# An attention and MLP block on one core: 84 five-pattern tiles made of two patterns, and nearly all shifts put on GpSimd in batches

## The chip, the cores and the metric

The program runs on one NeuronCore of a Trainium2 chip. The metric is the device time of one execution in microseconds. The engines are called as in the profile: PE (TensorE), ACT (ScalarE), DVE (VectorE), POOL (GpSimd) and SP (SyncE, which issues most DMAs). Each runs its own list of instructions in order, and they wait for each other by semaphores.

## The reference

One block with two branches on the same normalised input: attention with 32 query heads of width 16 that share one key and one value head, and an MLP with a tanh GELU. There are 2048 rows of width 512; the MLP is 1792 wide.

```python
xn = _layernorm(x)
q = (xn @ wq).reshape(B, S, 32, 16).transpose(0, 2, 1, 3)
k, v = xn @ wk, xn @ wv
p = softmax(einsum("bhqd,bkd->bhqk", q, k) * 16 ** -0.5)
attn = einsum("bhqk,bkd->bhqd", p, v).transpose(0, 2, 1, 3).reshape(B, S, 512) @ wo
h = gelu(einsum("bsd,df->bsf", xn, w1) + b1)
out = x + attn + einsum("bsf,fd->bsd", h, w2) + b2
```

## The kernel before

**Tiles and units.** The scores are cut into 2048 tiles of 128 keys by 512 queries, one PSUM bank each. Three tiles make a unit; there are 683 units. PSUM holds two halves of three banks: while the tiles of one unit are turned into exponentials out of one half, PE writes the scores of the next unit into the other (L1069, three matmuls that take one 32-row group of the array each, so that they run together). A half is written again when every tile in it has been read.

**Two ways to an exponential.** A table of 683 letters (DTAB) says which tiles of a unit go to ACT and which to DVE. ACT reads its one to three tiles of a unit with one Exp (L1109) into the buffer E. DVE reads a tile with one instruction, called p1 in the code (L1140): it adds a constant to the f32 score, cuts it off at 64 and writes int16. Read as bf16, these bits are a rough exponential: the upper bits are the power of two, and the lower seven a straight line in place of the curve. The error is smoothed by summing five patterns: the same bits with -26, 0, 26, 51 and 77 added (SPL_K), each weighted by a constant that is put into its own copy of V (SPL_C, V1). So a tile of DVE costs four shifts, each an integer addition on a whole tile, and five matmuls with V where a tile of ACT costs one. The bits and their shifted copies lie in the buffer Dt: 19 places for first bits, and three times 11 for copies.

**Batches.** Up to six tiles of DVE are gathered, and then `close_batch` writes their shifts (L1182 to L1197). SPL_STEPS says for each kind of batch which shift goes to which engine: "p" is POOL, in pieces of at most two tiles (PL_N, L1186), with a 64-bit integer addition that treats four int16 at a time; "d" is DVE, over all tiles of the batch (L1193). A piece meant for POOL is done by DVE (L1161) where the planner finds that earlier (L389 to L393). The planner starts POOL's pieces only beside DVE instructions that aren't marked `lock` (L384 to L398).

**The products with V** (`pv_mm`, L1153) use 32 columns of the array each, so four run side by side, one per head of a group. They add into bank 6; bank 7 takes the projections of q, the MLP and the output projection in pieces, four column groups side by side as well (L749, L767) or as row pieces that ride on the score matmuls (L763).

**What sets the order.** The whole program is recorded first, and `Prog.schedule` then plays it through with costs of its own and writes the order of each engine. Its tables set costs (C_OCC, PL_OCC), due times of the side work (HP, YP, QK, Q3) and, for the preparation, the order of its instructions (PRO_DUE). `emit` adds a semaphore wait wherever an instruction needs another engine's result. The order is therefore fixed when the program is built; on the chip only the waits move.

**Stages.** Preparation (layer norm, transposes, k, v, the first q) until the first Exp; then the 683 units with all the side work between them, and two stretches in which ACT does GELUs (L1342, L1347); then the end: the last output rows (`y_last`, `o_norm_last`) and one store.

Of the kernel before, what the change touches and what calls it, by code (L numbers as in the profile page):

```python
# [5 lines left out]
dt = mybir.dt  # L6
# [31 lines left out]
P1_ALLOW = -20.0  # L38
EV_ALLOW = -2.0
S_WAIT = 0.1  # L40
P_WAIT = 0.0
PL_OCC = (0.398, 0.61)
PL_N = 2
ON_OCC = 0.66
PL_LAT = 0.06
PL_GATE = 0.1
PL_WIN = 0.4
PL_TAKE = 1.0
PL_DUE = 3.0
PL_START = 0.065  # L50
PL_SEM = 0.16
PL_FREE = 0.06
# [3 lines left out]
RH = ((0,0,1,1,0,0,1,0,1,1,0,1,0,1),(0,0,0,0,1,1,1,1,1,1,1,1,1,1),(0,1,0,0,1,0,0,1,1,0,0,0,2,0),(1,0,0,1,0,1,1,1,1,1,1,1,1,1))  # L56
RQ = ((1,1,1,1),(0,0,2,2),(1,0,2,2),(0,0,0,0))
RY = ((4,3,3,4),(4,3,4,2),(4,5,2,3),(4,4,2,5))
# [13 lines left out]
DMASK = {".": (), "0": (0,), "2": (2,), "a": (0, 1), "b": (1, 2), "x": (0, 1, 2),  # L72
         "o": (0,), "t": (2,), "A": (0, 1), "B": (1, 2), "X": (0, 1, 2),
         "p": (0,), "u": (2,), "C": (0, 1), "D": (1, 2), "Y": (0, 1, 2)}
CLOSE = "otABXpuCDY"
THREE = "puCDY"
DTAB = "o0t02o.Ct0u2...0p00o.u2..p00po0t00p0tu0202....2uttt2tu0..C.o202p.222t.0oo0pt.B.0upp.p.2o2p22.2p000pp2.22p0o2t222.uo00p000u2t2o022tt2t2u20.2p0o02222.u220u000u0u0o02o202o2o..2u0t0t2uttbXXxXDu2u.20u0p0o02p222puo02.A202.tu0p0p.ap.0up0oo0p.0u0t020u.p.0ob.22.a002.p.b.B2.t.up2.otpt02.C0.p0p0.o020u0p0t2utt2.2p0o0p.t0t0o0o0o00o.202ut.0p0t200p0pt2.u2u020uu2p2u0u0.02p2u20002o2p002.u0ut020o0.o000.u020p20ou.ooo2t..u0u.p22u2p.p.B2pb.2u2po0p2put0pp00u2p0o..22.oo..2u020p0op22222p..2u2p2u020p2t022t2t.2o0022u000.0p2t0o0puu0pbYxYYA2t2p2t2.o0t0t202220u2po220tpp0.0202p.2p0p022p2p0u0p200ut2u000.p020u0o2022p2o00.2p202utp0p2t0tpu0t0t.u..0pt0uo0p2ppu0o2ptoo.pt..uo0oppa.p2.p.pp.ppup...bb.t000tt.tp..."
YF = 671.2567
# [11 lines left out]
Q3 = (3.13604,15.59782,1.3122)  # L90
QK = ((79.39235,91.86289,161.48976),(89.43004,105.17994,147.29074),(107.14608,109.54065,152.86984))
HP = ((35.0394,106.61171,41.40498,24.75776,42.85696,74.69052,118.31736,29.75129,84.77514,90.16891,73.93822,12.90461,18.00252,59.26326),(53.1749,30.86375,13.60201,93.43062,56.91912,0,0,0,0,0,0,0,0,0),(249.98302,265.3673,301.57062,267.28344,332.95778,255.58795,276.31909,268.60694,288.87995,299.75237,231.3787,266.76069,464.96186,415.4469),(420.73779,406.30738,480.5553,448.48685,406.52914,0,0,0,0,0,0,0,0,0))
YP = ((216.91445,183.61894,219.257,200.80829),(342.24149,390.93758,358.11329,404.06844),(569.56343,516.05804,661.62593,615.81662),(590.23906,607.46323,652.09363,671.23592))
# [36 lines left out]
class Prog:  # L130
# [131 lines left out]
    def schedule(self):  # L262
# [12 lines left out]
        able = dict(ready)  # L275
# [34 lines left out]
        while left:  # L310
            best_e, best_t = None, None
            for e in engs:
# [3 lines left out]
                if not able[e] and not pro:  # L316
                    continue
# [1245 lines left out]
```

## Time and profile before

| | us |
|---|---|
| median of 3 runs | 719.8 (719.77 to 720.71) |
| span of the profiled execution | 718.4 |
| busy: PE, DVE, ACT, POOL | 705.1, 701.2, 704.2, 446.1 |
| ACT, all Exp instructions (L1109), 675 of them | 652.6 |
| DVE, p1 (L1140), 589 of them | 409.5 |
| DVE, shifts planned for it (L1193) and taken from POOL (L1161) | 155.9 and 96.3 |
| POOL, shifts (L1160), 659 of them | 424.1, idle ahead of them 251.2 |

The profile is of one execution, and its span is 1.4 us below the median of the runs. Busy time is what an engine spent on its instructions; on ACT and DVE an instruction's record overlaps the next one's by some 0.08 to 0.25 us, so what one costs is the distance from its start to the next one's. On PE four column matmuls run at once, and each record is about 0.38 us long though the next four start after 0.22. POOL's records include the time that an instruction stands still after its start.

### The profile page before, as it was taken

The numbers are of one execution on the slowest core, as the hardware profiler recorded it, in microseconds if no ns is written. First come the engines' busy times: TensorE is split into PE (matmuls) and PEld (weight loads), VectorE is DVE, ScalarE is ACT, GpSimd is POOL, SyncE is SP. The second block draws the span as 40 slices with busy tenths as digits, with TensorE's granted clock in tenths as the row PEclk, the third lists the DMA queues.
The fourth block names the chain that finished last, engine by engine and source line by source line (L and its number), as shares of the span: only waits on it lengthen the run. The fifth ranks groups of instructions, "written<-read, shape, count | busy, mean of one in ns | idle before, by whom it ended". The sixth has DMA issues, their size and how long they took to land.

```text
span 718.4 us, 22628 instructions
## 1 busy us (share of the span) xinstructions
PE 705.1 (98%) x9241; PEld 220.3 (31%) x9244; DVE 701.2 (98%) x1396; ACT 704.2 (98%) x761; POOL 446.1 (62%) x727
## 2 busy tenths in 40 slices
PE   7899999999999999999999999999999999999998
PEld 4332333222233233322322233232234222222332
DVE  8899999999999999999999999999999999999996
ACT  7899999999999999999999999999999999999997
POOL 8355555777665654566776754746875766765431
PEclk9999999999999999999999999999999999999999
DMA  9200100101020010110101011010110101111111
GB/s 302 86 10 17 33 10 18 26 10 25 13 41 20 18 39 17 23 42 16 26 18 32 24 40 26 21 22 15 28 24 18 19 22 26 32 23 31 28 30 41
DMA packets 36255, 23.60 MB, mean 33 GB/s; under 512 B 17768, under 2 KB 32568, under 8 KB 36152
## 3 DMA queue, kind: packets, MB, share of 16 engines
q1 hardware_dynamic: 34824, 21.86, 12.1%
q8 instruction: 74, 1.21, 0.7%
q10 hardware_dynamic: 1328, 0.30, 0.2%
q14 instruction: 29, 0.24, 0.1%
HBM read 13.28 MB, written 2.35 MB: 22 GB/s over the span
## 4 chain that ended last, share of the span: by engine, by line
ACT 49%; PE 46%; DVE 3%; DMA 1%; issue 0%; SPq 0%
ACT E L1109 49%; PE pAll L1153 23%; PE pAll L1085 14%; PE pAll L767 5%; PE pAll L749 3%; DVE stats L857 1%; DVE Dt L1140 1%; DMA x_sb<-in_A_x_dram 1%; DVE ub L894 0%; PE pAll L1523 0%; DVE xnT L920 0%; DVE ub L1319 0%; PE pAll L763 0%; DVE mv L871 0%; DVE Dt L1193 0%
## 5 line engine op out<-in xcount | busy, mean ns | idle before, releaser
L1109 ACT ACTIVATE E<-pAll 128x1024 bf16<-128x1024 f32 (+2 forms) x675 | 652.6, 1150 | 1.9 <-PE pAll L763 0.8
L1160 POOL INT64_ADD Dt<-Dt x659 | 424.1, 652 | 251.2 <-DVE Dt L1140 84.9
L1140 DVE TENSOR_SCALAR Dt<-pAll 128x512 int16<-128x512 f32 (+1 forms) x589 | 409.5, 713 | 5.8 <-PE pAll L763 3.8
L1153 PE MATMUL pAll<-Dt,V 128*32 128x512 bf16 x3120 | 414.0, 383 | 0.1
L1153 PE MATMUL pAll<-E,V 128*32 128x512 bf16 x1424 | 281.2, 385 | 0.0
L1085 PE MATMUL pAll<-QT,KT 32*128 32x512 bf16 x2048 | 266.9, 384 | 4.1 <-ACT E L1109 2.8
L1193 DVE TENSOR_SCALAR Dt<-Dt 128x1024 int16<-128x1024 int16 (+6 forms) x286 | 155.9, 556 | 0.3
L1085 PEld LDWEIGHTS pAll<-QT,KT 32*128 32x128 bf16 x2048 | 66.6, 90 | 275.5 <-ACT E L1109 258.5
L1153 PEld LDWEIGHTS pAll<-Dt,V 128*32 128x32 bf16 x3120 | 106.1, 94 | 111.6 <-issue 79.8
L1161 DVE TENSOR_SCALAR Dt<-Dt 128x1024 int16<-128x1024 int16 (+1 forms) x294 | 96.3, 357 | 0.0
L1153 PEld LDWEIGHTS pAll<-E,V 128*32 128x32 bf16 x1424 | 64.5, 94 | 48.5 <-issue 37.6
L767 PE MATMUL pAll<-xnT,w_sb 128*32 128x512 bf16 x544 | 78.0, 383 | 0.3 <-DVE ub L1319 0.3
L767 PE MATMUL pAll<-w_sb,ub 128*32 128x512 bf16 x336 | 51.2, 381 | 0.0
L763 PE MATMUL pAll<-w_sb,ub 32*128 32x512 bf16 x112 | 43.1, 384 | 0.1
L767 PE MATMUL pAll<-w_sb,x_sb 128*32 128x512 bf16 x300 | 42.8, 382 | 0.0
L767 PE MATMUL pAll<-wop,oTp 128*32 128x512 bf16 x192 | 36.2, 382 | 0.0
L763 PE MATMUL pAll<-w_sb,x_sb 32*128 32x512 bf16 x92 | 35.4, 384 | 0.0
L767 PEld LDWEIGHTS pAll<-xnT,w_sb 128*32 128x32 bf16 x544 | 20.4, 94 | 13.8 <-issue 8.4
L763 PE MATMUL pAll<-xnT,w_sb 32*128 32x512 bf16 x64 | 24.6, 384 | 0.0
L1319 DVE TENSOR_SCALAR ub<-pAll,b1T 128x512 bf16<-128x512 f32 x28 | 20.7, 740 | 0.1
L763 PE MATMUL pAll<-xnT,wq_sb 32*128 32x512 bf16 x52 | 20.0, 384 | 0.0
L749 PE MATMUL pAll<-xnT,w_sb 128*32 128x512 bf16 x288 | 18.8, 380 | 0.0
(135 smaller groups left out, 352.5 us busy)
## 6 DMA issues: line engine op xcount, KB each, us to landing
w_sb<-in_B_w_dram SPq DMA_DIRECT2D x2, 1792.0 KB, 14.1
OfP<-Of SPq DMA_DIRECT2D x96, 32.0 KB, 2.0
rbP<-rden_rows SPq DMA_DIRECT2D x96, 32.0 KB, 1.9
x_sb<-in_A_x_dram SPq DMA_DIRECT2D x16, 128.0 KB, 2.2
QT<-qp SPq DMA_DIRECT2D x124, 16.0 KB, 1.8
out_dram<-x_sb SPq DMA_DIRECT2D x15, 128.0 KB, 1.7
x_sb<-in_A_x_dram SPq DMA_DIRECT2D x7, 256.0 KB, 5.5
OfP<-Of SPq DMA_DIRECT2D x56, 16.0 KB, 1.9
```

Source lines behind the costliest of these rows:

```text
L749: add("pe", lambda e, c=c, j=j: e.matmul(o[c, :], l[:, c], rh, start=start, stop=stop, tile_position=(0, 32 * j)), r, [(k, j) for k in w] ...
L763: add("pe", lambda e, b, c=c, j=j: e.matmul(pM, l[c, :], rh[c, :], start=False, stop=b, skip_group_check=True, tile_position=(32 * j, 0)), ...
L767: add("pe", lambda e, b, c=c, j=j: e.matmul(pM[c, :], l[:, c], rh, start=n == 0, stop=b, skip_group_check=True, tile_position=(0, 32 * j)) ...
L857: dve(lambda e, ti=ti, c=c: e.bn_stats(stats[:, c, :], x_sb[:, ti, :]), r=[("x", ti)], w=[("st", ti)], n=511)
L1085: ins = e.matmul(o, l, rh, start=True, stop=True, tile_position=(q0, 0))
L1109: o = act(lambda e: e.activation(E[:, s0:s0 + na, :], bank(b0, na).rearrange("p (a n) -> p a n", a=na), ACT.Exp, scale=LN2 / 128.0), w=[B( ...
L1140: op = dve(lambda e: e.tensor_scalar(Dt[:, s:s + n, :], bank(bk, n).rearrange("p (a n) -> p a n", a=n), float(127 * 128) + SPL_D, SPL_MIN, ...
L1153: add("pe", lambda e, a, b: e.matmul(pO[32 * j:32 * j + 32, :], V1[:, v, kt, :], rhs, start=a, stop=b, tile_position=(0, 32 * j)), r=r + [ ...
L1160: return e.int64_add(d.bitcast(dt.uint64), x.bitcast(dt.uint64), k * 0x0001000100010001 % 2 ** 64)
L1161: return e.tensor_scalar(d, x, float(k), None, ALU.add)
L1193: dve(lambda e, d=view(o, nb), q=view(i, nb), k=k: e.tensor_scalar(d, q, float(k), None, ALU.add), r=keys(i), w=keys(o), n=nb * n * TBW, m ...
L1319: dve(lambda e: e.tensor_scalar(ubs[tb % 2][:, ft, :], pM, b1T[:, ft:ft + 1], None, ALU.add), r=["b1T"], w=M4 + [ukey(tb, ft)], n=TBW + 57 ...
```

## The change

**Two patterns.** Batches whose letter in the new table BTAB is S, T or U (39 batches, 84 tiles) are made another way. p1 adds another constant. Then DVE writes two parts of the bits with bit operations: the mantissa bits with a fixed exponent, a number m between 0.5 and 1, and the exponent bits alone, a power of two P. One product puts (first bits) x m in the place of the first bits. The sum of P and that product, 2^e (1 + (1 + f)^2 / 2), is the exponential up to a constant factor and a small error, so two matmuls with the plain V take the place of five. The other 544 tiles of DVE keep five patterns.

**All shifts on POOL.** The new SPL_STEPS give every shift to POOL but for 15 instructions of the kind "d" in the third variant. PL_N is 6, and a step may cover two neighbouring copies, so one POOL instruction now takes one to twelve tiles. DVE no longer takes shifts from POOL.

**Tables and planner.** DTAB, and with it the split between ACT and DVE, is new (ACT has 1420 tiles instead of 1424). PTAB sets the priority of each p1. A `lock` instruction of DVE is planned outside POOL's instructions; the first POOL instruction after one waits for it by a semaphore, but no `lock` instruction of DVE waits for POOL on that account. A few costs, the due times, and the order of the preparation are new.

```diff
-SPL_STEPS = (((1, 0, 1, 26, "p"), (2, 0, 2, 51, "d"), (0, 0, 1, -26, "p")),
-             ((1, 0, 1, 26, "p"), (2, 0, 1, 51, "d"), (3, 0, 1, 77, "p"), (0, 0, 1, -26, "p")))
+SPL_STEPS = (((1, 0, 1, 26, "p"), (2, 0, 1, 51, "p"), (3, 0, 1, 77, "p"), (0, 0, 1, -26, "p")),
+             ((1, 0, 1, 26, "p"), (2, 0, 2, 51, "p"), (0, 0, 1, -26, "p")),
+             ((1, 0, 1, 26, "p"), (2, 0, 2, 51, "d"), (0, 0, 1, -26, "p")))
+POST = (1.0, -1.0, 4.0)
+P1 = {".": -20.0, "a": 0.0, "b": 0.4, "c": 1.0}
+QUAD = 18
+QUAD_TS, QUAD_TT = 4, 2
+QUAD_D = 127 * 128 - 75.0461
...
-C_OCC = 0.197
+C_OCC = 0.2075
...
-PL_OCC = (0.398, 0.61)
-PL_N = 2
+PL_FIX, PL_TILE, PL_N = 0.1635, 0.2124, 6
...
         def seen(o):
             if o.kind == "rs":
                 return o.rdy + RS_MAX
-            return max(o.rdy + (PL_TAKE if o.kind == "pl" else 0.0), lockend) if o.lock else o.rdy
+            return max(o.rdy, dlock if o.eng == "pool" else lockend) if o.lock else o.rdy
...
-                if e == "dve" and op.kind == "pl":
-                    ready["pool"].remove(op)
-                    ready["dve"].append(op)
-                    op.eng = op.stream = "dve"
...
+                if e == "pool" and op.lock:
+                    if any(o.lock and o.rdy + LK_WAIT <= t for o in ready["dve"]):
+                        free["pool"] = max(free["dve"], t) + 0.01
                         continue
+                    lockend = t + op.occ
+                    if gate is not None:
+                        op.deps.append(gate)
+                        gate.need = True
+                        gate = None
+                if e == "dve" and op.lock:
+                    dlock, gate = t + op.occ + 0.18, op
...
+            quad = ord(plan[batch[0][0]]) - 65 >= QUAD
+            add_c = QUAD_D if quad else float(127 * 128) + SPL_D
...
+                for q in range(0, n, QUAD_TS):
+                    quad(lambda e, d, x: e.tensor_scalar(d, x, 0x7f, 0x3f00, ALU.bitwise_and, ALU.bitwise_or), q, min(QUAD_TS, n - q), (0,), 1, 4)
+                for q in range(0, n, QUAD_TS):
+                    quad(lambda e, d, x: e.tensor_single_scalar(d, x, -128, ALU.bitwise_and), q, min(QUAD_TS, n - q), (0,), 2, 4)
+                for q in range(0, n, QUAD_TT):
+                    quad(lambda e, d, x, y: e.tensor_tensor(d.bitcast(bf), x.bitcast(bf), y.bitcast(bf), ALU.mult), q, min(QUAD_TT, n - q), (0, 1), 0, 2)
+                for b in (2, 0):
+                    for q, (t, _) in enumerate(batch):
+                        gg, kt, j = tile_of(t)
+                        pv_mm(gg, j, 0, kt, Dt[:, slot(b) + q, :].bitcast(bf), [(("D", base[b > 0] + q), b)])
...
                 if eng == "p":
-                    for q in range(0, n, PL_N):
-                        w = min(PL_N, n - q)
-                        d, x = (Dt[:, slot(b) + q:slot(b) + q + w, :].rearrange("p a n -> p (a n)") for b in (o, i))
...
+                    for q in range(0, n if nb == 1 else 1, PL_N):
+                        w = min(PL_N, n - q) if nb == 1 else n
+                        d, x = (wide(b, nb, q, w) for b in (o, i))
...
+                        add("pool", lambda e, d=d, x=x, k=k: e.int64_add(d, x, k * 0x0001000100010001 % 2 ** 64), kx if o != i else [], kd,
+                            occ=PL_FIX + PL_TILE * nb * w, lat=PL_LAT, allow=PL_DUE, kind="pl", lock=True, after=[lib])
```

**What moves.** Three places. The first is POOL's list just after the preparation, from the load of the library with the 64-bit addition on (L1040 before, L1008 now). A tile counts 256 here, so 128x512 is two tiles and 128x2x1024 eight. Before:

```order
L1040 ISA
L1037 MEMSET b2row 128x512
L1160 ISA Dt<-Dt 128x256
L1160 ISA Dt<-Dt 128x512 x2
L1160 ISA Dt<-Dt 128x256
L1160 ISA Dt<-Dt 128x512 x4
L1160 ISA Dt<-Dt 128x256 x3
L1160 ISA Dt<-Dt 128x512 x3
```

Now:

```order
L1008 ISA
L1183 ISA Dt<-Dt 128x1024 x2
L1183 ISA Dt<-Dt 128x2x1024 x2
L1183 ISA Dt<-Dt 128x1024 x3
L1183 ISA Dt<-Dt 128x2x1024
L1183 ISA Dt<-Dt 128x1024 x2
L1183 ISA Dt<-Dt 128x768 x3
L1183 ISA Dt<-Dt 128x2x1024
```

Fourteen pieces of one or two tiles become fourteen of three to eight. Over the whole program POOL had 659 additions over 1162 tiles and now has 512 over 2108; the sizes of 512 elements and below fall from all 659 to 118 plain ones, and 110 of the new ones cover two blocks of Dt.

The second place is DVE's list some forty instructions ahead of its end, between the last tiles. L1140 and L1110 are p1, L1161 and L1193 shifts. Before:

```order
L1140 TENSOR_SCALAR Dt<-pAll 128x512 x2
L1193 TENSOR_SCALAR Dt<-Dt 128x2x2560
L1140 TENSOR_SCALAR Dt<-pAll 128x512 x2
L1161 TENSOR_SCALAR Dt<-Dt 128x1024
L1140 TENSOR_SCALAR Dt<-pAll 128x512 x2
L1161 TENSOR_SCALAR Dt<-Dt 128x1024
L1193 TENSOR_SCALAR Dt<-Dt 128x2x2048
```

Now, with the bit operations (L1164, L1166) and the product (L1168):

```order
L1110 TENSOR_SCALAR Dt<-pAll 128x512 x2
L1164 TENSOR_SCALAR Dt<-Dt 128x1024
L1110 TENSOR_SCALAR Dt<-pAll 128x512
L1166 TENSOR_SCALAR Dt<-Dt 128x1024
L1110 TENSOR_SCALAR Dt<-pAll 128x512
L1164 TENSOR_SCALAR Dt<-Dt 128x512
L1110 TENSOR_SCALAR Dt<-pAll 128x512
L1166 TENSOR_SCALAR Dt<-Dt 128x512
L1110 TENSOR_SCALAR Dt<-pAll 128x512
L1168 TENSOR_TENSOR Dt<-Dt 128x1024
```

The shifts between the p1 are gone and steps of two-pattern batches stand there; 21 of the 84 tiles belong to units 646 to 679. Over the whole program DVE loses 580 shifts, keeps 15 (L1186, 68 tiles) and gains 42 + 42 bit operations and 55 products.

The third place is the end of PE's list. `E,V` and `Dt,V` are products with V, `w_sb,x_sb` the last output rows of the MLP, `wop,xnT` and `xnT,oT` the output projection. Before:

```order
L1153 MATMUL pAll<-Dt,V 32x512
L749 MATMUL pAll<-w_sb,x_sb 32x512 x8
L1153 MATMUL pAll<-E,V 32x512 x2
L749 MATMUL pAll<-w_sb,x_sb 32x512 x30
L749 MATMUL pAll<-x_sb,ident 32x512 x4
L749 MATMUL pAll<-wop,xnT 32x512 x8
L749 MATMUL pAll<-xnT,oT 32x512 x16
```

Now:

```order
L1123 MATMUL pAll<-Dt,V 32x512
L717 MATMUL pAll<-w_sb,x_sb 32x512 x11
L1123 MATMUL pAll<-E,V 32x512 x2
L717 MATMUL pAll<-w_sb,x_sb 32x512 x41
L717 MATMUL pAll<-x_sb,ident 32x512
L717 MATMUL pAll<-wop,xnT 32x512
L717 MATMUL pAll<-x_sb,ident 32x512 x3
L717 MATMUL pAll<-wop,xnT 32x512 x4
```

Eleven more matmuls of the MLP now stand behind the last product with V. Over the whole program PE's products with V out of Dt fall from 3120 to 2888, those out of E from 1424 to 1420, and all full-width column matmuls from 6612 to 6352.

More of the change, by code (lines that the diff above doesn't have):

```diff
@@ L322, in schedule @@
             e, t = best_e, best_t
-            cand = [o for o in able[e] if (o.rdy if e == "pe" else seen(o)) <= t + 1e-9]
+            cand = [o for o in ready[e] if (o.rdy if e == "pe" else seen(o)) <= t + 1e-9]
             if e == "pe":
@@ L484, in schedule @@
             if op.kind == "S" and s_seen and (rider is None or rider.vis <= op.start):
[L485 removed]
+                rs = [o for o in ready["pe"] if o.kind == "rs" and o.tag in op.tag and o.rdy <= t + 1e-9]
                 if rs:
@@ L508, in schedule @@
                     o.nun -= 1
-                    v = q.vis if cross else q.end
+                    v = q.vis + (TO_POOL.get(q.eng, 0.0) if o.kind == "pl" and q.kind != "lib" else 0.0) if cross else q.end
                     if v > o.rdy:
@@ L1470, in bass_parallel_sum__grouped_kv_mqa__dense_activation_gelu__prompt_kernel @@
                 first, n = (t, 1) if n == 0 else (first, n + 1)
-                if n == KB or last_d[t // TPG] == t or (DTAB[t // 3] in CLOSE and not any(is_d[t + 1:t // 3 * 3 + 3])):
-                    three[first] = int(DTAB[t // 3] in THREE)
+                if n == KB or last_d[t // TPG] == t or (BTAB[t // 3] != "." and not any(is_d[t + 1:t // 3 * 3 + 3])):
+                    plan[first] = BTAB[t // 3] if BTAB[t // 3] != "." else "A"
                     bsize[first], n = n, 0
```

142 lines of the change are left out of this document (54 added, 88 removed).

## The prediction

> **What bounds the kernel now.** First the page's busy times, the granted clock, and the chain that ended last.
>
> ```profile
> PE 705.1 (98%) x9241; PEld 220.3 (31%) x9244; DVE 701.2 (98%) x1396; ACT 704.2 (98%) x761; POOL 446.1 (62%) x727
> ...
> PEclk9999999999999999999999999999999999999999
> ...
> ACT 49%; PE 46%; DVE 3%; DMA 1%; issue 0%; SPq 0%
> ```
>
> Three engines are busy 98% of the span, so busy time alone names no bound. The chain does more: 49% ACT and 46% PE, but 3% DVE. The end is handed to and fro between Exp and matmuls; DVE, as full as they are, rarely is what they wait for. The clock is full throughout.
>
> Next, ACT alone: the timeline (start, length, instruction), one stretch of it, and the groups by shape.
>
> ```profile
> 24.69 16.16 ACT L1109 ACTIVATE E<-pAll 128x1024 bf16<-128x1024 f32 x16
> 712.32 1.16 ACT L1271 ACTIVATE Of<-pAll,orow,mrow 128x256 f32<-128x256 f32 x2 [0.58 <-PE pAll L1153]
> 226.48 9.31 ACT L1109 ACTIVATE E<-pAll 128x1024 bf16<-128x1024 f32 x10
> L1109 ACT ACTIVATE E<-pAll 128x1536 bf16<-128x1536 f32 x4 | 5.6, 1603 | 0.0
> L1109 ACT ACTIVATE E<-pAll 128x1024 bf16<-128x1024 f32 x563 | 529.5, 1105 | 1.1 <-PE pAll L763 0.4 <-PE pAll L1085 0.2
> L1109 ACT ACTIVATE E<-pAll 128x1536 bf16<-128x1536 f32 x93 | 138.0, 1523 | 0.6 <-PE pAll L763 0.2 <-PE pAll L1085 0.2
> L1109 ACT ACTIVATE E<-pAll 128x512 bf16<-128x512 f32 x19 | 12.3, 646 | 0.3 <-PE pAll L763 0.2
> L1342 ACT ACTIVATE ub<-ub 128x3584 bf16<-128x3584 bf16 x4 | 12.8, 3193 | 0.0
> L1347 ACT ACTIVATE x_sb<-pAll,b1T 128x512 bf16<-128x512 f32 x18 | 11.1, 701 | 0.0
> L1342 ACT ACTIVATE x_sb<-x_sb 128x2560 bf16<-128x2560 bf16 x2 | 4.7, 2367 | 0.0
> L1342 ACT ACT_TABLE_LOAD x2 | 2.6, 1283 | 0.0
> L1357 ACT ACT_TABLE_LOAD x2 | 2.6, 1283 | 0.0
> ```
>
> From the first Exp (24.69) to the instruction behind the last (712.32) lie 687.6 us. Ten Exps of two tiles take 9.31; less the last one's own 1.2, nine steps of 0.90 (0.903 in what follows). Three tiles: (5.6 - 1.6) / 3 = 1.33. So a tile costs 0.43 and one alone about 0.48, an estimate from these two. ACT's own work is 563 x 0.903 + 93 x 1.33 + 19 x 0.48 = 641.2, and 33.8 for GELUs and table loads (the last five rows): 675.0. Some **12.6 us** of the 687.6 are steps drawn out by waiting, though the idle column shows hardly any, since one Exp's record covers the gap.
>
> Then PE, in a plain stretch and by its groups.
>
> ```profile
> 231.43 0.39 PE L1085 MATMUL pAll<-QT,KT 32*128 32x512 bf16 x3
> 231.75 0.40 PE L1153 MATMUL pAll<-E,V 128*32 128x512 bf16 x3
> 231.97 0.38 PE L767 MATMUL pAll<-wop,oTp 128*32 128x512 bf16 x1
> 232.29 0.39 PE L1085 MATMUL pAll<-QT,KT 32*128 32x512 bf16 x3
> ...
> L1085 PE MATMUL pAll<-QT,KT 32*128 32x512 bf16 x2048 | 266.9, 384 | 4.1 <-ACT E L1109 2.8 <-DVE KT L1015 0.2
> L1153 PE MATMUL pAll<-Dt,V 128*32 128x512 bf16 x3120 | 414.0, 383 | 0.1
> ```
>
> Scores start at 231.43, a round of four column matmuls at 231.75, the next at 231.97, scores again at 232.29: 0.32 from scores to columns, 0.22 a round, 0.32 from the last round back. There is no hole, and PE's idle time before 2048 score matmuls is 4.1 us in all, so some 5 with the small groups: PE runs at its own pace for about **682** of the 687.6 us, more than ACT's 675. Its least need would be 683 units x 0.64 = 437, and the column rounds past the first of a unit: 6612 / 4 + 16 short ones = 1669, less 683, x 0.22 = 217; together 654. The other 28 are rounds that aren't full. So PE is the longest chain by 7, ACT the next, and the main part is 5.6 longer than PE's 682, because each waits for the other now and then.
>
> **What the change does, part by part.**
>
> *Exps.* 580, 82 and 14 of two, three and one tiles (counted in the new order) instead of 563, 93 and 19: 523.7 + 109.1 + 6.7 = 639.5, that is **-1.7 us** on ACT, whose need becomes 673.3.
>
> *Matmuls.* The order has 260 full-width column matmuls fewer. If they leave as whole rounds, 65 x 0.22 = **14.3 us** leave PE, and its need falls to 668. From below: one that leaves a round whose others stay saves nothing, so 0. I take 14.3, since the removed ones are three of each two-pattern tile's five and most rounds are built of four at a time from whatever is ready. This changes which chain is longest: ACT's 673.3 is now ahead of PE's 668. With the same 5.6 on top the main part is 678.9, **8.7 us less** than 687.6. The ends of that: 1.7 (PE's rounds stay as many) and 14.3 (all 12.6 of waiting go, with the 1.7).
>
> *DVE.*
>
> ```profile
> L1140 DVE TENSOR_SCALAR Dt<-pAll 128x512 int16<-128x512 f32 (+1 forms) x589 | 409.5, 713 | 5.8 <-PE pAll L763 3.8 <-PE pAll L1085 1.0
> L1193 DVE TENSOR_SCALAR Dt<-Dt 128x1024 int16<-128x1024 int16 (+6 forms) x286 | 155.9, 556 | 0.3
> L1161 DVE TENSOR_SCALAR Dt<-Dt 128x1024 int16<-128x1024 int16 (+1 forms) x294 | 96.3, 357 | 0.0
> L1161 DVE TENSOR_SCALAR Dt<-Dt 128x512 int16<-128x512 int16 x130 | 33.4, 282 | 0.0
> L1193 DVE TENSOR_SCALAR Dt<-Dt 128x2048 int16<-128x2048 int16 x92 | 62.5, 681 | 0.0
> L1286 DVE TENSOR_TENSOR sqq<-qp 128x512 bf16<-128x512 bf16 x16 | 6.6, 410 | 0.0
> ```
>
> 252.2 us of shifts (the second and third rows) go. Added by the order: bit operations in four sizes, one to four tiles (20, 9, 6 and 7 of them, twice), priced like shifts of their size at 0.28, 0.41, 0.55 and 0.68: 35 us; products, 26 of one tile as L1286 at 0.41 and 29 of two at 0.68 (an estimate: 0.27 more for the second tile): 30; 15 shifts that stay: 11; four more tiles of p1: 3. DVE falls from 701 to about 528, 73%. No row shows a bit operation. From below they can't cost less than the shift of one tile each, 84 x 0.28 = 24; from above, at the rate of p1, 0.68 a tile, they are 168 tiles x 0.68 = 114. Even then DVE is at 607 of 718. I take the shift's price; either way DVE's size adds nothing to the sum, and what hides it is ACT's 673. By the chain's 3% the 173 us freed gain little by themselves.
>
> *POOL.*
>
> ```profile
> L1160 POOL INT64_ADD Dt<-Dt x659: 392/611/2037, 35.1 to 707.8; - x165
> 136.10 0.68 DVE L1193 TENSOR_SCALAR Dt<-Dt 128x2048 int16<-128x2048 int16 x1
> 136.70 0.68 DVE L1140 TENSOR_SCALAR Dt<-pAll 128x512 int16<-128x512 f32 x1
> 136.28 0.98 POOL L1160 INT64_ADD Dt<-Dt  x1 [0.92 <-DVE sqq L1286]
> 137.48 0.61 POOL L1160 INT64_ADD Dt<-Dt  x1 [0.23 <-DVE Dt L1140]
> ```
>
> An addition over one tile takes 0.39 (the least), over two 0.61 (the median): 0.173 and 0.219 a tile. The new order has 512 over 2108 tiles: 89 + 462 = 550 us, up from 114 + 254 = 368 without its standing still. The rows show what it shares with DVE: POOL's instruction at 136.28 takes 0.98, 0.61 longer than up to 136.67, which is about when DVE's shift gives way to the next instruction (136.70); beside p1 (137.48) it takes 0.61. So additions and DVE's 16-bit instructions exclude each other. In the new order those of DVE are 76 us, L1286's 6.6, and the 19 norms of about 11: with 550, **644 us**, and 112 separate stretches of them, each with a handover of 0.23 (the idle time at 137.48), 26: 670 of the 677 between POOL's first addition (35.1) and 712. It fits, by 7 us. I take it as hidden: late shifts only delay products that PE can take at any time, as long as Dt has free places. No row shows additions of more than two tiles or over two blocks. From below they cost 0.219 a tile and nothing else, 462; from above a large one costs as much as its pieces of two would, 0.305 a tile, 643, and POOL is 86 over. I take 550, since the fixed part is there in both rows and an instruction over more tiles starts only once; a rival goes part of the way to the upper end.
>
> *Preparation.* Its order is new on all engines, but the same instructions stand in it; the table load on ACT moves behind three DMA issues, and ACT has nothing to do until 4.6 us. I take 0, with 0.8 either way: the last copy of K (0.6 long) and its four matmuls can come before or after the first scores.
>
> *End.*
>
> ```profile
> 712.08 1.68 PE L749 MATMUL pAll<-w_sb,x_sb 128*32 128x512 bf16 x28
> 713.59 0.39 PE L749 MATMUL pAll<-x_sb,ident 128*32 128x512 bf16 x4
> 713.80 0.60 PE L749 MATMUL pAll<-wop,xnT 128*32 128x512 bf16 x8
> 714.33 1.21 PE L749 MATMUL pAll<-xnT,oT 128*32 128x512 bf16 x16
> ```
>
> Behind the last product with V, 28 matmuls take from 712.08 to 713.59, 0.054 each; eleven more make 0.6 us, of which 0.1 fits before the last projection (714.33). **+0.5**, from below 0.
>
> **Sum**: -8.7 + 0.5 = -8.2 on a span of 718.4, 710.2. The runs' median lies 1.4 above this span, outside of it nothing is changed: 719.8 - 8.2 = **711.6 us**.
>
> **The rivals.**
>
> *PE gives nothing back.* Rounds thin out but stay as many, or each half of PSUM is late because a round had just begun, whatever the load. Only Exps and the end change: 719.8 - 1.7 + 0.5 = 718.6. For it: the waits are small and everywhere, 12.6 us over 675 Exps. Against it: PE has no hole now. [...]
>
> *The waiting goes altogether*: 719.8 - 1.7 - 12.6 + 0.5 = 706.0.
>
> *Additions and DVE's 16-bit work become the bound.* Place: batches of four to twelve tiles on POOL, five patterns. With 7 us to spare over 2108 tiles it decides from 0.222 us a tile on; at 0.228, 4% more than the 0.219 read from one and two tiles, it is 12 us over the spare: copies come late, Dt's places stay taken, p1 waits, then scores and Exps: 711.6 + 12 = 723.6, **slower**. Against it: 0.39 and 0.61 hold a fixed part that larger pieces share.
>
> *DVE is held behind a long addition.* The new order has 189 DVE instructions that need what POOL has, POOL is at work 81% of the time with 1.07 us a piece, and none of them waits by a semaphore. Where the planner's times are off, DVE stands about 0.5 us, and p1, hence scores, behind it.
>
> ```profile
> 441.17 0.61 POOL L1160 INT64_ADD Dt<-Dt  x1 [1.99 <-PE pAll L1153]
> 441.59 0.47 DVE L1161 TENSOR_SCALAR Dt<-Dt 128x1024 int16<-128x1024 int16 x1
> 440.66 0.42 DVE L1161 TENSOR_SCALAR Dt<-Dt 128x1024 int16<-128x1024 int16 x1
> ```
>
> A shift that DVE started inside an addition took 0.47 instead of 0.42; today that is rare, as additions are short. The gain is gone from 16 of the 189 on (16 x 0.5 = 8); at 40, 711.6 + 20 is too much for a DVE that is 27% idle, so I price one in eight: 24 x 0.5 = 12, 723.6, slower. [...]
>
> **How the numbers follow.** Forecast 0.52; waiting gone 0.09; nothing given back 0.14; shared ports as the bound 0.13; DVE held 0.12. A measurement here can tell about 0.2%, 1.4 us, from no change: 718.6 is "same". Faster 0.52 + 0.09 = 0.61, same 0.14, slower 0.25. The forecast alone spans 708 to 716 (PE's 14.3 half or more, preparation 0.8). The range goes from 706.0, waiting gone, to 724.0, the two slow cases at their prices, and leaves out what lies beyond them, some 0.15: the upper end of POOL's additions above all.
>
> **What would show it.** Right: Exp steps of two tiles nearer to 0.903, main part near 679, PE with holes before scores, DVE near 73%, POOL near 550 busy, POOL named in no large wait of DVE or PE. Wrong: DVE 16-bit records far over 0.28 and 0.41 (held behind POOL); additions of four tiles over 173 + 4 x 219 = 1049 ns; p1 idle with PE's products as releaser (Dt full); or PE still without holes (rounds thinned).

## The result and the profile after

The changed kernel takes 725.07 us (median of 3 runs, 724.91 to 725.12) against 719.80: ratio 1.0069, interval 1.0049 to 1.0089. It is **slower by 0.7%**, and above the upper end of the predicted range. The profiled execution spans 723.3 us, 4.8 more than before (723.25 against 718.43).

Where the 4.8 us lie is read from the timeline of PE at four places: the scores of the first, the 13th and the last unit in the kernel before, then in the changed one (start, length, instruction).

```profile
24.25 0.39 PE L1085 MATMUL pAll<-QT,KT 32*128 32x512 bf16 x3 [0.23 <-DVE KT L1015]
35.17 0.39 PE L1085 MATMUL pAll<-QT,KT 32*128 32x512 bf16 x3
709.81 0.39 PE L1085 MATMUL pAll<-QT,KT 32*128 32x512 bf16 x2
```

```profile
27.42 0.39 PE L1053 MATMUL pAll<-QT,KT 32*128 32x512 bf16 x4 [1.34 <-DVE KT L983]
40.53 0.39 PE L1053 MATMUL pAll<-QT,KT 32*128 32x512 bf16 x3
714.13 0.39 PE L1053 MATMUL pAll<-QT,KT 32*128 32x512 bf16 x2
```

| stretch | before | after | difference |
|---|---|---|---|
| start to first scores | 24.25 | 27.42 | +3.17 |
| first to 13th unit | 10.92 | 13.11 | +2.19 |
| 13th to last unit | 674.64 | 673.60 | -1.04 |
| last scores to the end of the span | 8.62 | 9.12 | +0.50 |

So the whole loss lies in the first 40 us, and the 670 units behind them, for which the change was made, gain 1 us. The page (busy times, granted clock, chain that ended last):

```profile
PE 705.1 (97%) x9000; PEld 217.4 (30%) x9000; DVE 585.8 (81%) x981; ACT 703.2 (97%) x762; POOL 558.5 (77%) x580
...
PEclk8899999999999999999999999999999999999999
...
PE 60%; ACT 37%; DVE 1%; DMA 1%; POOL 1%; issue 0%; SPq 0%; POOLq 0%; DVEq 0%
```

DVE fell from 98% to 81%, POOL rose from 62% to 77%, PE and ACT are as busy as before. The clock row shows two eights at its start where the kernel before had only nines. The windows of PE alone show that closer (stretch, its length, PE's busy time, instructions, granted clock, DMA), first before, then after:

```profile
8.00:11.40 3.40, 2.98 (x20) 0.53 1.10 359
11.40:15.20 3.80, 3.48 (x55) 0.98 1.02 404
25.50:28.90 3.40, 3.06 (x39) 1.00 0.03 6
28.90:32.30 3.40, 3.03 (x33) 1.00 0.02 5
```

```profile
8.00:11.40 3.40, 2.01 (x14) 0.57 1.10 360
11.40:15.20 3.80, 3.69 (x36) 0.50 1.02 404
25.50:28.90 3.40, 0.81 (x8) 1.00 0.01 2
28.90:32.30 3.40, 2.93 (x23) 0.51 0.01 1
32.30:35.70 3.40, 3.40 (x31) 0.50 0.02 5
```

Before, PE is at half clock until some 11 us. After, it is so until 15.2, and once more from 28.9 to 35.7: in the stretch ahead of that, 25.5 to 28.9, PE worked for only 0.81 of 3.40 us, where it had worked for 3.06. At half clock scores and columns take 0.55 apart instead of 0.32 (timeline of PE after, to be held against the rows at 231 us in the prediction):

```profile
32.40 0.61 PE L1053 MATMUL pAll<-QT,KT 32*128 32x512 bf16 x3
32.95 0.62 PE L1123 MATMUL pAll<-E,V 128*32 128x512 bf16 x4
33.50 0.61 PE L1053 MATMUL pAll<-QT,KT 32*128 32x512 bf16 x3
```

The Exps are the 580, 82 and 14 of the new order, and their mean lengths are those of before within 4% (1115, 1538 and 671 ns). But three of them start late, far behind the first 40 us (timeline of ACT after):

```profile
61.50 1.02 ACT L1077 ACTIVATE E<-pAll 128x1024 bf16<-128x1024 f32 x1 [0.84 <-PE pAll L1123]
320.06 1.45 ACT L1077 ACTIVATE E<-pAll 128x1536 bf16<-128x1536 f32 x1 [0.66 <-PE pAll L1053]
366.21 1.02 ACT L1077 ACTIVATE E<-pAll 128x1024 bf16<-128x1024 f32 x1 [0.64 <-PE pAll L1053]
```

ACT stands idle for 2.1 us ahead of these three, the first time until products with V have run, then twice until the scores have. In the kernel before no Exp between 40 and 540 us waits for more than 0.3 us. By the distance of starts the three places cost 2.8 us.

What was new on DVE and POOL, in the groups by shape and in the view of the buffer Dt (least, median and greatest length):

```profile
L1164 DVE TENSOR_SCALAR Dt<-Dt 128x512 int16<-128x512 int16 x20 | 6.1, 307 | 0.1
L1168 DVE TENSOR_TENSOR Dt<-Dt 128x1024 bf16<-128x1024 bf16 x29 | 19.7, 689 | 0.2
L1168 DVE TENSOR_TENSOR Dt<-Dt 128x512 bf16<-128x512 bf16 x26 | 11.6, 445 | 0.1
```

```profile
L1183 POOL INT64_ADD Dt<-Dt x512: 399/1040/2746, 38.5 to 690.5; - x171
L1164 DVE TENSOR_SCALAR Dt<-Dt x42: 280/416/1764, 71.5 to 714.1; 128x512 int16<-128x512 int16 x20, 128x1024 int16<-128x1024 int16 x9, 128x2048 int16<-128x2048 int16 x7, 128x1536 int16<-128x1536 int16 x6
```

DVE's bit operations take what shifts of their size took (0.28 to 0.31 in the mean for a tile), the products 0.45 and 0.69. One bit operation stands out with 1.76 us (the greatest length of L1164), where others over four tiles take 0.68. POOL's additions have a median of 1.04 us, which is what a piece of four tiles takes, and 536 us in all.

### The profile page after: what moved, and what is told of

Read it like the earlier page. It is cut to its first block, busy times and chain, and to the rows that moved or that the text cites. A ratio compares the mean times of both kernels' runs of the same rounds, so it can differ in the third digit from the quotient of the medians.

```text
span 723.3 us, 21591 instructions
## 1 busy us (share of the span) xinstructions
PE 705.1 (97%) x9000; PEld 217.4 (30%) x9000; DVE 585.8 (81%) x981; ACT 703.2 (97%) x762; POOL 558.5 (77%) x580
## 4 chain that ended last, share of the span: by engine, by line
PE 60%; ACT 37%; DVE 1%; DMA 1%; POOL 1%; issue 0%; SPq 0%; POOLq 0%; DVEq 0%
ACT E L1077 34%; PE pAll L1123 28%; PE pAll L1053 19%; PE pAll L735 8%; PE pAll L717 2%; ACT ub L1335 1%; DMA x_sb<-in_A_x_dram 1%; PE pAll L711 1%; ACT x_sb L1340 1%; PE pAll L731 1%; POOL Dt L1183 0%; DVE Dt L1110 0%; PE pAll L881 0%; DVE stats L825 0%; ACT x_sb L1335 0%
## 5 line engine op out<-in xcount | busy, mean ns | idle before, releaser
L1077 ACT ACTIVATE E<-pAll 128x1024 bf16<-128x1024 f32 (+1 forms) x676 | 651.4, 1157 | 6.0 <-PE pAll L1053 3.4
L1183 POOL INT64_ADD Dt<-Dt x512 | 536.2, 1067 | 124.9 <-DVE Dt L1168 27.6
L1110 DVE TENSOR_SCALAR Dt<-pAll 128x512 int16<-128x512 f32 (+1 forms) x600 | 421.6, 712 | 116.1 <-PE pAll L731 59.3
L1123 PE MATMUL pAll<-Dt,V 128*32 128x512 bf16 x2888 | 385.4, 384 | 1.5 <-POOL Dt L1183 0.6
L1123 PE MATMUL pAll<-E,V 128*32 128x512 bf16 x1420 | 257.9, 387 | 0.6 <-DVE Of L1232 0.5
L1123 PEld LDWEIGHTS pAll<-Dt,V 128*32 128x32 bf16 x2888 | 95.6, 94 | 117.2 <-issue 80.6
L1123 PEld LDWEIGHTS pAll<-E,V 128*32 128x32 bf16 x1420 | 59.3, 94 | 46.1 <-issue 35.1
L1168 DVE TENSOR_TENSOR Dt<-Dt 128x1024 bf16<-128x1024 bf16 (+1 forms) x55 | 30.7, 574 | 0.3
L731 PE MATMUL pAll<-xnT,w_sb 32*128 32x512 bf16 x80 | 30.8, 385 | 0.0
L735 PE MATMUL pAll<-xnT,wq_sb 128*32 128x512 bf16 x204 | 19.2, 397 | 0.0
```

Source lines behind the costliest of these rows:

```text
L731: add("pe", lambda e, b, c=c, j=j: e.matmul(pM, l[c, :], rh[c, :], start=False, stop=b, skip_group_check=True, tile_position=(32 * j, 0)), ...
L735: add("pe", lambda e, b, c=c, j=j: e.matmul(pM[c, :], l[:, c], rh, start=n == 0, stop=b, skip_group_check=True, tile_position=(0, 32 * j)) ...
L1077: o = act(lambda e: e.activation(E[:, s0:s0 + na, :], bank(b0, na).rearrange("p (a n) -> p a n", a=na), ACT.Exp, scale=LN2 / 128.0), w=[B( ...
L1110: op = dve(lambda e: e.tensor_scalar(Dt[:, s:s + n, :], bank(bk, n).rearrange("p (a n) -> p a n", a=n), add_c, SPL_MIN, ALU.add, ALU.max), ...
L1123: add("pe", lambda e, a, b: e.matmul(pO[32 * j:32 * j + 32, :], V1[:, v, kt, :], rhs, start=a, stop=b, tile_position=(0, 32 * j)), r=r + [ ...
L1168: quad(lambda e, d, x, y: e.tensor_tensor(d.bitcast(bf), x.bitcast(bf), y.bitcast(bf), ALU.mult), q, min(QUAD_TT, n - q), (0, 1), 0, 2)
```

## The experiments

All runs by groups; the table behind them has the measurements, the lengths of the stretches being those of the profiled execution of each run. In the text a run goes by the first part of its label (e1a, e2). Fillers are matmuls on zeros whose result nobody reads.

### The first 40 us

In the first two runs only fillers are added to the changed kernel's finished order: ahead of the first transposes, and around the first scores.

```diff
+extra_fill(pr, pr.pro_filler, pr.ops.index(pes[k0]), 24, pr.fill_deps)   # e1a
+extra_fill(pr, f6, pr.ops.index(ss[2]), 12, ss[0].deps)                  # e1b
+extra_fill(pr, f6, pr.ops.index(ss[0]), 12, pr.fill_deps)                # e1b
```

> 24 matmuls on zeros more on PE, ahead of the first transposes (PE stood from 5.3 to 8.9 us); nothing else differs from the changed kernel. Theory 1 (the clock: the new order of the preparation lets PE stand or work too little, its granted clock is 0.50 until 15.2 us instead of 11.2, and 0.50 again from 29.0 to 35.6): the clock is full before 12 us, the transposes and K matmuls of 11 to 16 us take half as long, the first Exp comes at 25.5 to 26.5 instead of 27.9, and the time is 722.5 to 724. Theory 2 (rows arrive later and the order on DVE and POOL is worse; the clock only goes with it): first Exp at 27.9, time 725.

> 12 matmuls on zeros ahead of the first scores and 12 behind the scores of the second unit (PE stood for 1.3 us in each place); nothing else differs from the changed kernel. Theory 1: first Exp at 27.9 as before, but no half clock from 29 to 35.6; scores of the eleventh unit at 36.5 instead of 38.6, and the time is 722.5 to 723.5. Theory 2: the first units are slow for lack of work, fillers change nothing, 725 or a little more.

> Both sets of matmuls on zeros. Theory 1: the sum of the two gains, 720 to 722, first Exp near 26, clock full from 12 us on. Theory 2: 725.

The late fillers bring 1.8 us, as theory 1 had it: full clock from 25.5 on, and 11.33 instead of 13.11 us to the 13th unit. The early ones bring 0.4, less than the runs can tell apart, and leave the first Exp where it was; but PE fell back to half clock behind them (0.65 from 11.4 to 15.2), so they didn't decide. Both together (e1c) bring no more than the late ones, 723.24, not the sum that theory 1 expected. A run that keeps the clock full decides.

```diff
+k1 = [o for o in pes if o.fn is not pr.pro_filler][4]
+extra_fill(pr, pr.pro_filler, pr.ops.index(k1), 8, pr.fill_deps)
```

> As the run with both sets of matmuls on zeros, and eight more behind the first four transposes, where PE stood again. Theory 1a (the part of the clock in the 3.2 us by which the first Exp is late): with the clock at full from 8 to 16 us the first Exp comes at 25.5 to 26.5 and the time is 721 to 722. Theory 2a (the 3.2 us are the order on ACT, DVE and POOL and the later first rows): the first Exp stays at 27.7 to 28.1 and the time at 723.2.

The windows of PE and the first Exp in this run:

```profile
8.00:11.40 3.40, 2.65 (x27) 1.00 1.10 361
11.40:15.20 3.80, 2.96 (x39) 1.00 1.02 401
25.50:28.90 3.40, 3.19 (x30) 1.00 0.04 8
```

```profile
27.67 3.28 ACT L1077 ACTIVATE E<-pAll 128x1536 bf16<-128x1536 f32 x3 [1.81 <-PE pAll L1053]
```

The clock is full from 8 us on, and the first Exp is still 3.0 us later than before (27.67 against 24.69): theory 2a. The early half clock cost 0.2 us at most (27.86 in the changed kernel and 27.73 in e1b, both without these fillers). The chain of waits shows where the time goes, with the last transposes and the first steps behind them in the kernel before, and then with the steps up to PE's last products in this run:

```profile
19.47 0.40 PE pAll L913 x4
19.89 0.60 ACT xnT L918
20.49 0.28 ACT KT L931
...
```

```profile
20.47 0.33 PE pAll L881 x5
20.82 1.08 ACT xnT L886 x2
...
22.11 0.28 ACT KT L899
...
22.44 1.08 PE pAll L711 x5
...
23.54 0.61 ACT KT L899
...
24.19 1.04 PE pAll L711 x4
```

The last transposes end 0.93 us later (20.80 against 19.87). Behind them, it took 4.4 us to the first scores before, and takes 6.4 now: two copies of K on ACT and two groups of products on PE (five and four) stand in the chain one behind the other, where the old order had one copy of K and small DVE work. The last of these moves can be seen in PE's list, in the kernel before and then in the changed one:

```profile
22.28 0.27 PE L1007 MATMUL pAll<-ident_f,kmx 128*1 128x128 f32 x1
22.70 0.39 PE L743 MATMUL pAll<-xnT,oTp 128*128 128x512 bf16 x1
```

```profile
24.39 1.04 PE L711 MATMUL pAll<-xnT,oTp 128*128 128x512 bf16 x4 [0.55 <-ACT KT L899]
25.27 0.27 PE L975 MATMUL pAll<-ident_f,kmx 128*1 128x128 f32 x1
```

The maxima of K (kmx), which the scores need, went through PE ahead of the four products of the last copy of K; now these four stand ahead of them, and wait for the copy before. What each of the moves costs was not tried. That it is the order is shown from both sides, by the table of due times alone:

```diff
-PRO_DUE = (1311.0639,1363.5356,1028.5148,655.8387,-9000,
...
+PRO_DUE = (19.99,-92.94,20.03,40.9,-30.58,52.22,4.66,
...
```

(this is e5; e2 is the same edit the other way on the kernel before.)

> The kernel before with nothing but the new table of due times for the preparation. Theory 1 and theory 2 (the loss is in the preparation): the first Exp comes about 3 us later than in the kernel before and the time is 723 to 725.5. Theory 3 (the preparation costs nothing by itself, the loss comes from the 683 units): 719.8.

> The changed kernel with the table of the preparation's due times of before. Theory 1 or 2 (the whole loss lies up to the 12th unit): the first Exp comes at 24.7, no half clock behind it; the 683 units gain 1 us and the end loses 0.5, so 719 to 720. Theory 3 (the units themselves lose): 723 or more.

e2 makes the kernel before as slow as the changed one, 724.80, with the first Exp at 27.66 and half clock behind it. Over all runs the first scores come at 23.87 to 24.84 with the old order of the preparation and at 27.01 to 27.77 with the new one. e5 didn't come out as expected: the first Exp is at 24.37, but the planner starts from another state and gives the units another order, which fell to half clock at 25.5 and took 675.43 from the 13th unit (the late Exp at 61.50 of the changed kernel has its counterpart at 59.16, and ACT is idle for 2.5 us ahead of it). So the last run leaves the units' order alone: each engine's instructions ahead of the first scores are put into the old order after planning.

```diff
+graft(pr, s0)     # the old order of the preparation, for every engine
+extra_fill(pr, f6, pr.ops.index(ss[2]), 12, ss[0].deps)
```

> The changed kernel's finished order, in which only the preparation stands in the order of before (with its matmuls on zeros), and 12 matmuls on zeros behind the scores of the second unit; from the first scores on every engine has the changed kernel's order. If the loss lies in the preparation and its clock, and the 683 units keep their 1 us: first Exp at 24.4 to 24.8, clock full behind it, from the 13th to the last scores 673.6 to 673.8, and the time is 719.0 to 720.2, as before or a little less. If the units lose something as well that the late start hides: 721 or more.

720.05, ratio 0.9996 (0.9987 to 1.0005): the loss is gone, and what is left of the change can't be told from nothing. No version here that leaves nothing out beats the kernel before.

### The units: less work for PE, DVE and POOL

These take instructions out of a finished order; whoever waited for one waits for what it had waited for. e3, e6, e7, e8 and e10 start from the kernel before, e4 from the changed one.

```diff
+drop(pr, pick_rounds(pr, 65))                                              # e3
+drop(pr, [o for o in pr.ops if o.kind == "post" and o.eng == "dve"][60:])  # e6
+drop(pr, gone)          # e7: rounds right ahead of late Exps
+ahead(pr, late)         # e8: scores put ahead of the last round
+drop(pr, [x[0] for x in pr.log if len(x) == 2 and x[1]])                   # e4
```

> The kernel before, from whose finished order 65 whole rounds (260 matmuls of Dt with V, spread over the run, each round behind another column round) are taken out; the rest stands in the same order. The products left out are missing in the result. Theory A (PE is the longest chain by 7 us and gives its time back, as the prediction had it): 711.5 to 713.5, about 7 us less. Theory B (Exps are late because of the steps around each unit, whatever the number of rounds): 718.5 to 720, not more than 1.4 us less.

> The kernel before, from whose finished order all but the first 60 of DVE's 580 shifts (some 227 us of DVE) are taken out; the products stay and use what lies in the copies. Theory D2 (DVE is hidden, as the chain's 3% says): 719.5 to 720.3, as the kernel before. Rival (DVE at 98% holds p1 and with it the scores): 716 or less.

> The kernel before; from its finished order the column round that stands right ahead of the scores is taken out where the trace of before shows the Exp behind these scores late by over 15 ns and the round holds only products with V: 102 rounds, 408 matmuls, which are missing in the result. Theory B1 (Exps wait for scores that a round right ahead of them has made late, whatever the number of rounds elsewhere): the waiting there, some 6.7 us, goes for the most part: 713 to 716.5. Theory B2 (the lateness is in the hand-over between Exp and scores itself): 719 to 720.3.

> The kernel before with nothing left out: at 138 units with a late Exp and two or more rounds ahead of their scores, the scores are put ahead of the last of these rounds. Theory B1: these Exps come in time and the moved rounds fit behind, 714 to 718.5. Theory B3 (the next scores are late in their place): 719.3 to 721.5.

> The changed kernel without the shifts by -26 that POOL makes in place, a quarter of its work (163 additions); the products that use them take the unshifted bits. Theory C (POOL's additions and DVE's 16-bit work hold up the products, as the rival had it): the 683 units get 3 us or more shorter, 722 or less. Theory D (POOL is hidden): 724.7 to 725.3, as the changed kernel.

None of the three reliefs of the kernel before is worth more than 0.5 us between the 13th and the last unit (674.57, 674.43 and 674.15 against 674.64), and the changed kernel doesn't feel a quarter of POOL's work either (674.12 against 673.60). To move scores ahead costs 3.3 us in that stretch, and 723.66 is more than either theory had: the Exps that were late gain some 3 us by the starts in the trace, and those of the two units behind them lose more than twice as much. But one full engine hides what another gives back, so two were relieved at once:

> The kernel before, from whose finished order three things are taken out together: all but the first 60 of DVE's shifts (227 us), the column rounds right ahead of late Exps, and every further round of four Dt products that stands behind another round: 798 column matmuls in all. Theory A2 (PE and DVE are both full, and each held the time when only the other was relieved): from the 13th to the last scores 668 us or less instead of 674.6, time 713 or less. Theory B2 (the Exps' own pace and their hand-over with the scores set the time; neither PE nor DVE does): 673.5 to 674.6, time 718.8 to 720.

The chain of waits of e3, e7 and e10:

```profile
ACT 74%; PE 22%; DVE 2%; DMA 1%; issue 1%; SPq 0%
```

```profile
ACT 77%; PE 17%; DVE 4%; DMA 1%; issue 0%; SPq 0%
```

```profile
ACT 86%; PE 12%; DVE 1%; DMA 1%; issue 0%; SPq 0%
```

ACT's share of the chain rises from 49% to 74, 77 and 86%, and the time stays. In e10 the stretch is even longer, 675.38 and above what theory B2 had, since PE, with so little to do in the second GELU stretch, fell to half clock:

```profile
544.00:548.00 4.00, 2.86 (x60) 1.00 0.08 21
548.00:552.00 4.00, 2.32 (x20) 0.72 0.17 35
552.00:556.00 4.00, 4.00 (x30) 0.50 0.14 24
```

With PE and DVE relieved 86% of the chain is ACT's: **in this order Exps and their hand-over need some 674 us by themselves**.

### The units: less work for ACT

```diff
-o = act(lambda e: e.activation(E[:, s0:s0 + na, :], bank(b0, na)...
+cw = na * TBW - (48 if na == 2 and u >= 40 else 0)
+o = act(lambda e: e.activation(E[:, s0:s0 + na, :]...[:, 0:cw], bank(b0, na)[:, 0:cw],
```

> The kernel before; 530 Exps of two tiles read and write 976 of their 1024 columns, the rest of the result is wrong; the finished order is the same. ACT needs 530 x 0.040 = 21 us less (0.427 us for 512 columns, from the steps of 0.903 and 1.33). Theory B2 (the Exps and their hand-over set the time, PE's missing holes are only a sign that its order was packed to fit): the units get 12 to 21 us shorter, 699 to 708. Theory A2 (PE and DVE are full as well, PE needs some 682 of the 687.6 us): not more than 6 us shorter, 714 or more.

> The changed kernel with the same cut in 544 Exps, 22 us less for ACT. Theory B2: 703 to 713, 12 to 22 us less. If PE's steps bind once ACT is faster, it falls by as much as the kernel before does and a few us more, since DVE has 17 points more room and PE 260 matmuls less: what the change sets free is then worth something only behind a faster ACT.

My theory B2 fell here: of 21 us taken from ACT only 2.0 come back (672.63), and of 22 in the changed kernel 3.0 (670.58). Of the few us more that I expected there, 1.0 came. Busy times and chain of e11, then of e12:

```profile
PE 704.3 (98%) x9241; PEld 221.8 (31%) x9244; DVE 699.6 (98%) x1396; ACT 694.1 (97%) x761; POOL 445.8 (62%) x727
...
PE 86%; DVE 9%; ACT 3%; DMA 1%; issue 0%; SPq 0%
```

```profile
PE 702.6 (98%) x8998; PEld 217.0 (30%) x9000; DVE 586.0 (81%) x981; ACT 691.8 (96%) x762; POOL 558.6 (78%) x580
...
PE 85%; DVE 4%; POOL 4%; ACT 4%; issue 1%; DMA 1%; SPq 0%; DVEq 0%
```

Now PE holds 86 and 85% of the chain. So ACT and PE are two chains of nearly equal length; whether a third stands behind them was the last question:

> The kernel before with the shortened Exps (21 us less of ACT) and the 798 column matmuls of the two sets of rounds out (some 200 rounds, 40 us of PE); DVE keeps its shifts. Theory E (ACT with its hand-over and PE with its steps are two chains of nearly the same length, so that only relieving both shortens the run): the units get 10 to 21 us shorter than before, 699 to 710. Theory F (something else, the hand-over or DVE at 98%, is just behind): 714 to 718.

> The same, and DVE's shifts out as well (227 us). Theory E: as the run without DVE's part, within 1.5 us of it. Theory F with DVE as the next chain: this run alone is shorter by 8 us or more.

Busy times and chain of e13, then of e14:

```profile
PE 681.1 (95%) x8446; PEld 213.2 (30%) x8446; DVE 698.2 (98%) x1396; ACT 692.9 (97%) x761; POOL 446.2 (62%) x727
...
DVE 59%; PE 32%; ACT 5%; issue 2%; DMA 1%; SPq 0%; DVEq 0%
```

```profile
PE 668.3 (95%) x8446; PEld 200.6 (29%) x8446; DVE 539.1 (77%) x876; ACT 685.6 (98%) x761; POOL 392.5 (56%) x727
...
ACT 62%; PE 29%; DVE 7%; DMA 1%; issue 0%; SPq 0%
```

There is a third, as theory F had it. With ACT and PE relieved DVE takes 59% of the chain and the stretch is 671.66; with DVE relieved too it is 657.49, 17 of the 21 us, and the run 702.93 (0.9766, 0.9749 to 0.9782). e14 is e10 with the short Exps, so it also shows that ACT held e10: 17.9 of 21 us come back. Two things soften the 671.66. Some of e13's and e14's time is half clock in the second GELU stretch (granted clock 0.50 and 0.65 from 548 to 556 us in e13, 0.92 and 0.65 from 536 to 544 in e14), and e13's profiled execution took 717.70 us where the three others took 714.71 to 715.00, so that 669 to 670 is nearer to its median. From the 201st to the 501st unit, ahead of that stretch, the kernel before takes 291.3 us, the changed one 291.2, e11 290.5, e13 289.1 and e14 282.8. ACT and DVE relieved together, with PE's rounds left in, was not run on the kernel before; e12 comes nearest, with DVE at 81%.

### What was measured

| run | us | ratio to before (interval) | first scores | to 13th unit | 13th to last |
|---|---|---|---|---|---|
| before (profiled) | 719.80 | | 24.25 | 10.92 | 674.64 |
| changed | 725.07 | 1.0069 (1.0049-1.0089) | 27.42 | 13.11 | 673.60 |
| e1a | 724.65 | 1.0066 (1.0051-1.0081) | 27.63 | 12.40 | 673.73 |
| e1b | 723.31 | 1.0049 (1.0032-1.0066) | 27.29 | 11.33 | 673.71 |
| e1c | 723.24 | 1.0045 (1.0030-1.0060) | 27.56 | 11.33 | 673.71 |
| e1d | 723.19 | 1.0048 (1.0033-1.0063) | 27.23 | 11.32 | 673.74 |
| e2 | 724.80 | 1.0068 (1.0053-1.0083) | 27.22 | 13.23 | 674.68 |
| e5 | 722.50 | 1.0034 (1.0021-1.0046) | 23.93 | 12.43 | 675.43 |
| e9 | 720.05 | 0.9996 (0.9987-1.0005) | 24.05 | 11.43 | 673.72 |
| e3 | 720.04 | 1.0002 (0.9993-1.0012) | 23.90 | 10.91 | 674.57 |
| e6 | 719.74 | 0.9997 (0.9987-1.0006) | 23.87 | 10.92 | 674.43 |
| e7 | 719.51 | 0.9993 (0.9983-1.0002) | 24.28 | 10.85 | 674.15 |
| e8 | 723.66 | 1.0053 (1.0038-1.0068) | 24.78 | 10.91 | 677.90 |
| e4 | 725.05 | 1.0071 (1.0056-1.0086) | 27.77 | 12.27 | 674.12 |
| e10 | 720.63 | 1.0004 (0.9995-1.0013) | 24.15 | 10.85 | 675.38 |
| e11 | 718.00 | 0.9972 (0.9961-0.9983) | 24.19 | 10.91 | 672.63 |
| e12 | 721.52 | 1.0021 (1.0012-1.0031) | 27.01 | 13.07 | 670.58 |
| e13 | 714.92 | 0.9937 (0.9918-0.9957) | 24.84 | 10.85 | 671.66 |
| e14 | 702.93 | 0.9766 (0.9749-0.9782) | 24.00 | 10.85 | 657.49 |

## Why the prediction was wrong

**The preparation** was put at 0, with 0.8 either way, "the same instructions stand in it". This is the step that decides the sign: it and what it triggers cost 5.4 us (3.17 and 2.19). The order of the preparation is worth 3.0 us (e1d against before; e9 takes it back), and the low use of PE around the first scores (0.81 of 3.40 us), behind which the granted clock was 0.51 and 0.50 for 6.8 us, some 1.8 (e1b); the rest is 0.4 us up to the 13th unit, which e9 keeps (11.43; the order of the first units or the fillers, not told apart), and the early half clock. The 0.8 allowed for the last copy of K and its four matmuls; of these the matmuls, with the copy that they wait for, take 1.7 us of the chain (23.54 to 25.23 in e1d). The prediction read the clock as full throughout from the page's row of nines, where one digit is 18 us, and looked at no window of the first 25 us.

**Matmuls, -8.7 us with the Exps**, failed as well. "PE is the longest chain by 7" and that the removed ones "leave as whole rounds" were both wrong. Of 65 rounds some 38 left (1839 before, 1801 after, with starts within 0.06 us counted as one round), as the rounds' mean fill fell from 3.63 to 3.56; the count is rough, since it finds 47 fewer in e3, from which 65 were taken. And e3, with its 65 whole rounds out, gains nothing. PE's missing holes were read as a sign that PE was the longer one; but the order is made by a planner that fills whatever room there is up to the next scores. ACT's 12.6 us of steps drawn out were counted as waiting for PE, and are nearly all still there when PE and DVE have little to do: the steps of all Exps add up to 655.0 us before and 655.7 in e10, with a need of 641.2. Of the time that is its own I can name one part: behind a one-tile Exp (0.48 us) the next Exp starts late, by 0.2 to 0.5 us in 13 places: 3.6 us in all before, 3.8 in e10. That the short Exp doesn't cover the scores behind it is my reading; the rest stays open.

What binds the units of the kernel before is three chains: ACT with its hand-over at some 674 us, PE's steps at 672.6 (e11, by the chain's 86%), DVE at 669 to 670 (e13). The change takes 17 points off DVE, 2% of its rounds off PE and 1.7 us off ACT. A gain of 1.0 us fits the least of these, but no run shows that it sets it, for the three late Exps after (61.50, 320.06 and 366.21) take part of it. They stand in e9 too, and there the steps of all Exps add up to 654.8 us, with a need of 639.5: the need is 1.7 less than before, and the sum 0.2. What the units would gain without these three places was not run. The rival "PE gives nothing back" had -1.7 for the units, near the 1.0. Of its two reasons, that rounds thin out but stay is borne out in part (some 27 of 65 stayed), and a round just begun ahead of the scores was not what held them (e7).

**DVE** was right in its price (bit operations 36.6 us against 35, products 31.3 against 30, a second tile taking 0.24 more where it had estimated 0.27: 0.689 against 0.445) and in adding nothing. Busy time is 586 and not the 528 of the sum because the records of neighbours overlap: in the trace of before, what is not a shift covers 511 us by itself, and not 701 - 252 = 449.

**POOL** was right: 536 us against 550, four tiles 1.04 against 1.05, and hidden (e4). No run shows the shared ports that the chances name; what the runs show is how long additions and DVE's 16-bit instructions took beside each other. As a bound the two rivals did not occur: bit operations of one tile took 0.28 to 0.31 in the mean, not over 0.4. But single records show the second one at work. The bit operation of 1.76 us started at 218.66, 0.25 us into an addition that ran from 218.41 to 219.88. With nine more such records, a product of one tile among them (0.90 instead of 0.42), that makes some 3 us on a DVE that is idle for 19% of the span.

**End**: +0.5 against +0.5, right.

With the preparation's 5.4 in place of 0 and the units' -1.0 in place of -8.7 the sum gives 719.8 + 5.4 - 1.0 + 0.5 = 724.7. Of the 0.4 that are left 0.3 lie in where it starts: executions of the kernel before that take 719.8 us have a span of 718.1, and the profiled one, with 718.4, ran some 0.3 longer, so the 1.4 between span and run should have been 1.7.

## What to carry to other kernels

Where several engines are 98% busy, no hole on one of them and no share of a chain says what relieving it is worth: in the kernel before the gain was held to that of the least relieved of three chains of nearly equal length, and runs with work taken out of the finished order, engine by engine and then together, tell them apart. A change that comes with a new order for the start is two changes: the first 40 us are read window by window, with the clock, on their own. A planner's order that left PE thin for some 3 us paid for it here with half clock in the next 3 to 7 (0.81 of 3.40 us busy, then 0.51 and 0.50 for 6.8 us in the changed kernel; 2.23 of 3.40, then 0.51 for 3.5 us in e5).

## What the runs showed of the hardware

The granted clock halved behind stretches in which PE did little: 0.81 of 3.40 us (25.5 to 28.9) in the changed kernel, 2.32 of 4.00 (548 to 552, already at 0.72) in e10. It came back 6.8 us later in the changed kernel (0.51 and 0.50 from 28.9 to 35.7), although PE was busy for most of that time (2.93 and 3.40 of 3.40), and in e10 it was 0.50 from 552 to 556, with PE busy for 4.00 of 4.00, and 0.93 from 556 to 560. How little is too little these runs don't settle: in e14 a stretch with 2.54 of 4.00 us (532 to 536) was followed by a granted clock of 0.92, and the next with 2.65 by 0.65. That taking work from PE can cost time in this way was new to me: e10's units took 675.38 us instead of 674.64, though its run can't be told from the kernel before (1.0004). So was that 24 fillers in one idle place only moved the half clock to the next one (e1a: 1.00 from 8.0 to 11.4, then 0.65 up to 15.2), and eight more behind them kept it away (e1d: 1.00 in both stretches).
